# Filter bank and hardswish block on one core: small units run inside a last-stage chunk's matmuls, first-stage units in other steps, GpSimd's sums of x behind them

## The chip, the cores and the metric

One of the eight NeuronCores of a Trainium2 chip runs the kernel. The metric is the time of one execution on the device in microseconds (us), the median over repeated executions. The engines are called PE (TensorE), DVE (VectorE), ACT (ScalarE), POOL (GpSimd) and SP (SyncE); PEld is TensorE's loading of weights.

## The reference

```
X = np.fft.rfft(x, axis=1)                     # x: (8, 3008, 256) float32
Y = X * (filt_r + 1j * filt_i)[None, :, :]     # filter: (1505, 256)
y = np.fft.irfft(Y, n=3008, axis=1).reshape(24064, 256)
h = y @ w_in                                   # (256, 2048)
g = h * np.clip(h + 3.0, 0.0, 6.0) / 6.0
out = g @ w_out                                # (2048, 256)
```

## The kernel before

**The two halves of the work.** The Fourier part takes each of the 8 images (3008 rows of 256 values) as a 47 x 64 grid. A *first-stage* unit (`a_unit` for image 1, `a6_unit` for images 2 to 7) multiplies columns of the grid with a 47-point transform; its sums and differences go to DRAM (`z_tmp`). `t2_load` brings them back transposed, `b_unit` transforms along the 64, `f_unit` (three products on DVE) and `y_unit` (one subtraction and one addition on DVE) apply the filter, and `bi3_unit` transforms back along the 64 for three results `y` at a time and stores to DRAM (`g_tmp`). The *last stage* takes chunks of five columns (235 pairs of rows): `t4_load` brings a chunk, `n_five` multiplies it with the inverse 47-point transform, 40 small matmuls into two PSUM banks, and `ring` copies the result (ACT, L686) into a ring of three blocks, `xn`. The dense part takes blocks of 512 rows of the result, 47 of them, each in 8 steps of 256 of the 2048 hidden values.

**A step of the dense part.** From block 1 on both products are done with seven instead of eight block products. They need sums of x, which POOL makes once per block (`t_sums`, seven operations at L760, reading `xn`, when a chunk has completed the block), and sums of g, which DVE makes. A step is, in PE's order: product A11 into the bank `al` and S1, A12 into the bank `be` (`up_1`); two matmuls of the step before's down product; S2 into `al`, S4 into `be` (`up_2`); four down matmuls; S3 (`up_3`); four down matmuls; A22 into `al` (`up_5`); four down matmuls, of which the last two need `g_last`. ACT copies what was in `al` and `be` (L775, L776 in `up_1`, L785 in `up_2`, L804 in `up_5`) before the next product adds to it, and makes `relu(0)` and `relu(1)` (L809). DVE adds (L790, L795), makes g (`hswish`, L814, twice per step) and its sums (L821, L822, and `g_last`, L827). At a block's end `out_1` to `out_5` put the output together, with two operations in step 0 and three in step 1 on DVE, and one on POOL.

**Where the Fourier units stand.** PE, DVE, ACT, POOL and SP each take their instructions in the order in which the program records them. A table `plan` says which units a step holds, at one of three places: 0 (`EARLY`: after A12; among them `n_five` and `b_unit`), 1 (between the down matmuls before A22 and A22 itself; `a6_unit`, `bi3_unit`) and 2 (the end of the step: sums, stores, loads). A unit at place 1 may use `be`, because L790 has read it by then. For image n with first block `first[n]` (5, 11, 17, 23, 29, 35, 41), places are counted in steps from the beginning of block `first[n] - 5`; this count is called the offset here. The `bi3_unit`s of images 2 to 7 stand at offsets 11, 16, 27, 32, f_units at 2, 3, 6, 7, 12, 13 and 16 more, y_units at 4, 5, 10, 11, 14, 15 and 16 more, b_units with every other f_unit. The first-stage units stand in steps counted from two blocks earlier: `A_AT = (4, 6, 10, 12, 14, 15)`, five units of six columns and one (the last) of two. n_fives stand where the blocks need them, mostly in steps 0, 1, 4 and 6 of a block.

**Units on a quarter of the array.** `n_five`, `a6_unit` and `bi3_unit` use 48 to 64 rows and 64 columns of the array, so four of their matmuls occupy four quarters (two row halves, two column halves). An `a6_unit` of six columns and a `bi3_unit` are three rounds of four products of 256 columns into two PSUM banks of the pool `psF` and the bank `be`. The two row halves must not write the bank `be` at once; so DVE copies two elements from it after the first round (`tensor_copy(out=t[:, 2, 1, 0:2], ...)`, L483, and L601), and the second use of the bank waits for that copy. A float32 product stands in the profile as two weight loads and two matmuls, its two passes.

**Stages in time.** The stages of image n+1 run beside the dense part of image n, so nearly all the run is one sequence of steps with units in them. `late(i)` decides whether `g_last` comes before or after the up product's sums: after in steps 1 and 2 of a block and behind a step with a unit of `HEAVY`.

Of the kernel before, what the change touches and what calls it, by code (L numbers as in the profile page):

```python
# [37 lines left out]
HC = NC // 2  # L38
XC = 4
NB = HC // XC  # L40
SIX = tuple(range(0, HC, 6))
TC = 4
NT = KH // TC
TB = 3
# [138 lines left out]
def kernel(  # L183
# [198 lines left out]
    def x_at(b, c):  # L382
        if b == 1:
            return xs[:, (b * NB + c) % 3, :, :], c * XC, XC
        t = xs.rearrange("p i j d -> p (i j) d")
        return t[:, ds((b * len(SIX) + c) % 2 * 6, 6), :], SIX[c], min(6, HC - SIX[c])

    def x_load(b, c):
        t, c0, n_ = x_at(b, c)
# [70 lines left out]
    def a_sums(b, c):  # L460
# [5 lines left out]
        nc.vector.tensor_tensor(out=t[:, :, 1, :], in0=t[:, :, 0, :], in1=ps, op=ALU.subtract)  # L466
        nc.vector.tensor_tensor(out=t[:, :, 0, :], in0=t[:, :, 0, :], in1=ps, op=ALU.add)

    def a6_unit(b, c):
        xc, c0, n = x_at(b, c)  # L470
        n //= 2
        t = t3p.tile([P, 3, 2, D], FP32, name="t3") if n == 3 else t1p.tile([P, 2, 2, D], FP32, name="t1")
        banks = [psF.tile([P, 512], FP32, name="psf", tag="f") for h in range(2)]
        be = psU.tile([P, 512], FP32, name="be") if n == 3 else None
        for r in range(n):
            for g in range(2):
                for h in range(2):
                    j, ps, o = (2, be, h) if r == 2 - 2 * h and n == 3 else (r - h if n == 3 else 0,) + (banks[h], r - h if n == 3 else 0)
                    q = g * n + j
                    nc.tensor.matmul(ps[ts(g, 64), ts(o, D)], wa[ds(h * 64, NA), ds((c0 + q) * 2 * KH, 64)],  # L480
                                     xc[ds(h * 64, NA), q, :], start=True, stop=True)
            if n == 3 and r == 0:
                nc.vector.tensor_copy(out=t[:, 2, 1, 0:2], in_=be[:, D:D + 2])  # L483
        m = min(n, 2)
        two = [ps[:, 0:m * D].rearrange("p (j d) -> p j d", d=D) for ps in banks]
        nc.scalar.activation(out=t[:, 0:m, 0, :], in_=two[0], func=AXT.Copy)
        if n == 3:
                nc.scalar.activation(out=t[:, 2, 1, 2:D], in_=be[:, D + 2:], func=AXT.Copy)
        st["t1", b, c] = t, be, two[1], n

    def a6_sums(b, c):
        t, be, ps, n = st["t1", b, c]
        v, m = nc.vector, min(n, 2)
        if n == 3:
            v.tensor_tensor(out=t[:, 2, 0, :], in0=be[:, 0:D], in1=t[:, 2, 1, :], op=ALU.add)
            v.tensor_tensor(out=t[:, 2, 1, :], in0=be[:, 0:D], in1=t[:, 2, 1, :], op=ALU.subtract)
        v.tensor_tensor(out=t[:, 0:m, 1, :], in0=t[:, 0:m, 0, :], in1=ps, op=ALU.subtract)
        v.tensor_tensor(out=t[:, 0:m, 0, :], in0=t[:, 0:m, 0, :], in1=ps, op=ALU.add)

    def z6_store(b, c):  # L500
        t, _, _, n = st.pop(("t1", b, c))
        for g in range(2):
            for ri in range(2):
                p0 = g * 64 + ri * KH
                nc.gpsimd.dma_start(z_d[b, :, ri, ds(SIX[c] + n * g, n), :, :].rearrange("k j s d -> k (j s d)"),
                                    t[p0:p0 + KH, 0:n, :, :].rearrange("p j s d -> p (j s d)"))

    def z_store(b, c, q=nc.gpsimd):
# [80 lines left out]
    def bi3_unit(b, i):  # L589
        ys = [st.pop(("y", b, i + v)) for v in range(3)]  # L590
        c = psU.tile([P, 512], FP32, name="be")
        banks = [psF.tile([P, 512], FP32, name="psf", tag="f") for ri in range(2)]
        t = t3p.tile([P, 3, 2, D], FP32, name="t3")
        to = [t[:, q, :, :].rearrange("p u d -> p (u d)") for q in range(3)]
        for r in range(3):
            for v in range(2):
                for ri in range(2):
                    x, u, ps, o = (2, v, c, ri) if r == 2 * ri else (v, r - 1 + ri, banks[ri], r - 1 + ri)
                    nc.tensor.matmul(ps[ts(v, 64), ts(o, D)], wi[ts(ri, 64), 0, :], ys[x][ts(ri, 64), u, :], start=True, stop=True)  # L599
            if r == 0:  # L600
                nc.vector.tensor_copy(out=to[2][:, 0:2], in_=c[:, 0:2])  # L601
        nc.scalar.activation(out=to[1], in_=banks[1], func=AXT.Copy)
        st["t3", b, i] = t
        st["bi3"] = to[0], banks[0], to[2], c

    def bi3_copies():
        if "bi3" in st:
            to, ps, third, c = st.pop("bi3")
            nc.scalar.activation(out=to, in_=ps, func=AXT.Copy)
            nc.vector.tensor_copy(out=third[:, 2:512], in_=c[:, 2:512])  # L610
# [54 lines left out]
    def t4_load(i):  # L665
# [8 lines left out]
        for c in range(2):  # L674
            for hh in range(2):
# [2 lines left out]
                                  bass.AP(tensor=g_d.tensor, offset=g_d.offset + ((b * NC + j) * 2 + c) * KH * D,  # L678
                                          ap=[[D, KH], [-2 * KH * D, NJ], [1, D]]))

    def ring(i, a, m_, to, out, src):
        done = 0
        while done < m_:
            r = (chunks[i][0] * HC * NA + to + done) % RING
            m = min(m_ - done, RING - r)
            nc.scalar.activation(out=out(ds(r, m)), in_=src[:, :, ds(a + done, m)], func=AXT.Copy)  # L686
            done += m

    def ready(i):
        t, n = pair(i)  # L690
        if (t + n) // PAIRS > t // PAIRS > 0:
            t_sums(t // PAIRS)


    def n_five(i):
        b, js, o, n = chunks[i]
        s0 = i % 2 * NJ
        ps = [psF.tile([P, 512], FP32, name="psn", tag="f")[:, 0:2 * n].rearrange("p (e n) -> p e n", e=2) for c in range(2)]
        for q, j in enumerate(js):
            for dh in range(2):  # L700
                for g in range(2):
                    for c in range(2):
                        r = ds(c * HALF, ATOM)
                        nc.tensor.matmul(ps[c][ts(g, HALF), dh, ts(q, NA)], t4[r, s0 + q, ds(dh * P + g * HALF, HALF)],  # L704
                                         groups[r, j, :], start=True, stop=True)
# [267 lines left out]
    EARLY = (a_unit, b_unit, bi_unit, n_unit, n_five)  # L973

    def at(step, fn, *a):
        plan.setdefault((step, 0 if fn in EARLY else 1 if fn in (w_scale, bi3_unit, a6_unit) else 2), []).append((fn, a))

    with tc.manual_schedule():

# [134 lines left out]
        stored = 0  # L1114
# [34 lines left out]

        at(n_at[TAIL - 2] + 1, lambda: nc.sync.dma_start(edge, wai_d[:, ds(NW + ND, ND)]))  # L1150
# [2 lines left out]
        for n in range(1, B):  # L1153
            a_at, f_at, y_at, bi_at = places(n)
            for c, s in enumerate(a_at):
                at(s, a_unit if n == 1 else a6_unit, n, c)
# [24 lines left out]
        HEAVY = (f_unit, y_unit, a_sums, n_five, a6_sums, bi3_unit)  # L1181
# [106 lines left out]
```

## Time and profile before

| | |
|---|---|
| median of 4 runs | 2643.12 us (2641.83 to 2644.22) |
| the profiled execution | 2644.22 us, its span 2642.4 us |
| granted TensorE clock | 1.00 |
| DMA | 198.29 MB moved, mean 75 GB/s |
| PE po L843, the down products | 43% of the chain that ended last |
| PE al and be L764, the up products | 42% of the chain |
| PE psn L704, n_five | 2% of the chain |

The span is what the profiler saw of the program; the time of the execution holds some 2 us more. In the rows of a group the columns are line, engine, operation, tile written <- tiles read, shape and count, then busy time, mean ns of one, and idle time before them. The chain lists pieces of work in order of time, with start and length in us.

### The profile page before, as it was taken

The numbers are of one execution on the slowest core, as the hardware profiler recorded it, in microseconds if no ns is written. First come the engines' busy times: TensorE is split into PE (matmuls) and PEld (weight loads), VectorE is DVE, ScalarE is ACT, GpSimd is POOL, SyncE is SP. The second block draws the span as 40 slices with busy tenths as digits, with TensorE's granted clock in tenths as the row PEclk, the third lists the DMA queues.
The fourth block names the chain that finished last, engine by engine and source line by source line (L and its number), as shares of the span: only waits on it lengthen the run. The fifth ranks groups of instructions, "written<-read, shape, count | busy, mean of one in ns | idle before, by whom it ended". The sixth has DMA issues, their size and how long they took to land.

```text
span 2642.4 us, 54927 instructions
## 1 busy us (share of the span) xinstructions
PE 2625.9 (99%) x21920; PEld 2337.8 (88%) x21920; DVE 2047.5 (77%) x3611; ACT 1296.4 (49%) x2677; POOL 485.5 (18%) x711
## 2 busy tenths in 40 slices
PE   8999999999999999999999999999999999999999
PEld 6598988989889898889988898888988889999998
DVE  7878867887678876788767887688877878766666
ACT  4554454444544444444444444545445454454554
POOL 2242021120211102111021210211112120111110
PEclk9999999999999999999999999999999999999999
DMA  8732234112241132411233112331123311110000
GB/s 241 223 90 79 58 99 116 53 32 85 77 116 52 32 85 81 112 52 36 81 86 107 53 37 80 89 104 53 56 61 89 104 56 48 48 43 23 19 21 25
DMA packets 130710, 198.29 MB, mean 75 GB/s; under 512 B 21602, under 2 KB 97472, under 8 KB 130262
## 3 DMA queue, kind: packets, MB, share of 16 engines
q1 hardware_dynamic: 115165, 150.12, 20.5%
q0 software_dynamic: 14720, 44.16, 6.1%
q8 instruction: 173, 2.83, 0.4%
q14 instruction: 83, 0.68, 0.1%
q10 hardware_dynamic: 569, 0.50, 0.1%
HBM read 122.43 MB, written 83.98 MB: 78 GB/s over the span
## 4 chain that ended last, share of the span: by engine, by line
PE 96%; DMA 2%; DVE 1%; issue 0%; ACT 0%; SPq 0%; POOL 0%; POOLq 0%; DVEq 0%; ACTq 0%
PE po L843 43%; PE al L764 24%; PE be L764 18%; PE psn L704 2%; PE psf L539 1%; PE psf L480 1%; PE po L886 1%; PE psf L599 1%; PE be L599 1%; PE be L480 1%; DMA w_all<-in_x_dram 1%; DMA g_tmp<-t 1%; PE al L875 0%; PE be L875 0%; PE psf L453 0%; PE psn L715 0%
## 5 line engine op out<-in xcount | busy, mean ns | idle before, releaser
L843 PEld LDWEIGHTS po<-w_all,g 128*128 128x128 f32 x10276 | 1370.4, 191 | 106.9 <-issue 10.4
L843 PE MATMUL po<-w_all,g 128*128 128x128 f32 x10276 | 1393.9, 276 | 1.0 <-DVE g L814 0.6
L809 ACT ACTIVATE r<-h,half_c 128x512 f32<-128x512 f32 x736 | 531.0, 721 | 334.6 <-DVE h L790 322.5
L764 PE MATMUL al<-xt,w_all 128*128 128x256 f32 x2208 | 659.6, 381 | 0.1
L814 DVE SCALAR_TENSOR_TENSOR g<-r,h 128x512 f32<-128x512 f32 x736 | 534.1, 727 | 147.5 <-ACT r L809 132.3
L764 PE MATMUL be<-xt,w_all 128*128 128x256 f32 x1472 | 437.8, 379 | 0.0
L790 DVE TENSOR_TENSOR h<-be,s 128x512 f32<-128x512 f32 x368 | 253.7, 689 | 144.7 <-PE be L764 136.1
L764 PEld LDWEIGHTS al<-xt,w_all 128*128 128x128 f32 x2208 | 335.4, 192 | 1.0 <-issue 0.5
L760 POOL TENSOR_TENSOR xt<-xn 128x256 f32<-128x256 f32 x184 | 149.6, 833 | 905.6 <-ACT xn L686 871.7
L764 PEld LDWEIGHTS be<-xt,w_all 128*128 128x128 f32 x1472 | 279.7, 190 | 37.9
L804 ACT ACTIVATE h<-al 128x256 f32<-128x256 f32 x368 | 141.4, 384 | 297.2 <-PE al L764 297.2
L795 DVE TENSOR_TENSOR h<-al,s 128x256 f32<-128x256 f32 x368 | 156.1, 424 | 155.9 <-PE al L764 152.9
L822 DVE TENSOR_TENSOR g<-g 128x512 f32<-128x512 f32 x367 | 261.3, 712 | 12.6
L785 ACT ACTIVATE s<-al 128x256 f32<-128x256 f32 x368 | 141.4, 384 | 214.4 <-PE al L764 212.9
L764 PE MATMUL al<-xn,w_all 128*128 128x256 f32 x736 | 226.4, 389 | 0.0
L776 ACT ACTIVATE s<-be 128x256 f32<-128x256 f32 x368 | 141.4, 384 | 171.0 <-PE be L764 171.0
L764 PE MATMUL be<-xn,w_all 128*128 128x256 f32 x736 | 218.9, 379 | 0.0
L821 DVE TENSOR_TENSOR g<-g 128x256 f32<-128x256 f32 x367 | 165.0, 450 | 12.6
L775 ACT ACTIVATE s<-al 128x256 f32<-128x256 f32 x368 | 141.1, 383 | 64.8 <-PE al L764 64.8
L827 DVE TENSOR_TENSOR g<-g 128x256 f32<-128x256 f32 x367 | 160.2, 437 | 2.4
L764 PEld LDWEIGHTS be<-xn,w_all 128*128 128x128 f32 x736 | 139.8, 190 | 18.9
L764 PEld LDWEIGHTS al<-xn,w_all 128*128 128x128 f32 x736 | 111.4, 191 | 24.7 <-issue 22.3
(170 smaller groups left out, 1849.1 us busy)
## 6 DMA issues: line engine op xcount, KB each, us to landing
t<-g_tmp SPq DMA_DIRECT2D x184, 120.0 KB
t<-z_tmp SPq DMA_DIRECT2D x42, 512.0 KB
g_tmp<-t POOLq DMA_DIRECT2D x68, 256.0 KB, 4.3
z_tmp<-t POOLq DMA_DIRECT2D x120, 144.0 KB, 3.4
o_tmp<-o SPq DMA_DIRECT2D x46, 256.0 KB
xs<-in_x_dram SPq DMA_DIRECT2D x60, 192.0 KB
ft<-in_filt_r_dram SPq DMA_DIRECT2D x168, 64.0 KB
ft<-in_filt_i_dram SPq DMA_DIRECT2D x168, 64.0 KB
```

Source lines behind the costliest of these rows:

```text
L760: nc.gpsimd.tensor_tensor(out=o, in0=x0, in1=x1, op=op_)
L764: nc.tensor.matmul(ps, w_in[p][:, w, :], x, start=start, stop=stop, skip_group_check=True)
L776: nc.scalar.activation(out=s5, in_=be[:, 1, :], func=AXT.Copy)
L785: nc.scalar.activation(out=s[:, 1, :], in_=al, func=AXT.Copy)
L790: nc.vector.tensor_tensor(out=st["h"][0].rearrange("p (a n) -> p a n", a=2), in0=be, in1=s, op=ALU.add)
L795: nc.vector.tensor_tensor(out=st["h"][1][:, 256:512], in0=al, in1=s5, op=ALU.add)
L809: nc.scalar.activation(out=r, in_=st["h"][i], func=AXT.Relu, bias=half_c, scale=1.0 / 6.0)
L814: nc.vector.scalar_tensor_tensor(out=st["g", k, p][:, o:o + 2, :].rearrange("p a n -> p (a n)"), in0=st["r", i], scalar=1.0, in1=st["h"][i ...
L821: v.tensor_tensor(out=g[:, G1, :], in0=g[:, G3, :], in1=g[:, G22, :], op=ALU.add)
L822: v.tensor_tensor(out=g[:, G3:G2 + 1:2, :], in0=g[:, G3:G1 + 1, :], in1=g[:, G11:G11 + 1, :].broadcast_to([P, 2, 256]), op=ALU.subtract)
L827: nc.vector.tensor_tensor(out=g[:, G4, :], in0=g[:, G12, :], in1=g[:, G2, :], op=ALU.subtract)
L843: nc.tensor.matmul(st["po", k][bank][:, part, u, :], g[:, a, ts(u, P)], w_out[p][:, w, :], start=(p == 0 and n in OPENS and u == 0), stop= ...
```

## The change

A small unit is now one product per quarter of the array, two per row half: `a2_parts` (the two-column first-stage unit) and `bi1_parts` (one `y` instead of three). `five_and` records it inside an `n_five`: the unit's two products for one row half, beside eight of the chunk's products for the other half; then 24 of the chunk's products for both halves; then the unit's two products for the other half, beside the chunk's last eight. The unit's results go to the bank `be`, with DVE's two-element copy between its halves. Such a chunk stands at place 1 instead of 0. Its copies into `xn`, and for `bi1` one copy out of `be` on DVE, are recorded in `bi3_copies`, after A22 and `relu(1)`; `t_sums` is recorded there too, or, where the chunk stands in step 1 of a block (and no chunk three steps on), at place 2 three steps later.

The six-column units are now numbers 0 to 3 and 5 (`SIX`), the two-column one is number 4, at 12, with a chunk; numbers 3 and 5 stand at 13 and 15, which are steps 5 and 7 of a block. Of the four `bi3_unit`s of an image one is taken apart: single ones stand at offsets 9, 16 and 25 (image 6: 9, 16, 17; image 7: 9, 11, 16), those of three at 14 (image 7: 20), 27 and 32. Before, in images 2 to 7, all twelve `y` went in threes at 11, 16, 27 and 32. In all other `bi3_unit`s and in the `a6_unit`s the order of the products inside a round is changed: the two of one row half, then the two of the other.

```diff
...
-SIX = tuple(range(0, HC, 6))
+SIX = (0, 6), (6, 6), (12, 6), (18, 6), (24, 2), (26, 6)
...
+    def a_product(ps, g, o, xc, c0, q, h):
+        nc.tensor.matmul(ps[ts(g, 64), ts(o, D)], wa[ds(h * 64, NA), ds((c0 + q) * 2 * KH, 64)],
+                         xc[ds(h * 64, NA), q, :], start=True, stop=True)
     def a6_unit(b, c):
         xc, c0, n = x_at(b, c)
         n //= 2
-        t = t3p.tile([P, 3, 2, D], FP32, name="t3") if n == 3 else t1p.tile([P, 2, 2, D], FP32, name="t1")
+        t = t3p.tile([P, 3, 2, D], FP32, name="t3")
         banks = [psF.tile([P, 512], FP32, name="psf", tag="f") for h in range(2)]
-        be = psU.tile([P, 512], FP32, name="be") if n == 3 else None
+        be = psU.tile([P, 512], FP32, name="be")
         for r in range(n):
+            for h in (1, 0):
+                for g in range(2):
+                    j, ps, o = (2, be, h) if r == 2 - 2 * h else (r - h, banks[h], r - h)
+                    a_product(ps, g, o, xc, c0, g * n + j, h)
+            if r == 0:
+                nc.vector.tensor_copy(out=t[:, 2, 1, 0:2], in_=be[:, D:D + 2])
+        two = [ps.rearrange("p (j d) -> p j d", d=D) for ps in banks]
+        nc.scalar.activation(out=t[:, 0:2, 0, :], in_=two[0], func=AXT.Copy)
+        nc.scalar.activation(out=t[:, 2, 1, 2:D], in_=be[:, D + 2:], func=AXT.Copy)
+        st["t1", b, c] = t, be, two[1], n
+    def a2_parts(b, c):
+        xc, c0, n = x_at(b, c)
+        t = t1p.tile([P, 2, 2, D], FP32, name="t1")
+        be = psU.tile([P, 512], FP32, name="be")
+        st["t1", b, c] = t, be, None, 1
+        def part(h):
             for g in range(2):
-                for h in range(2):
-                    j, ps, o = (2, be, h) if r == 2 - 2 * h and n == 3 else (r - h if n == 3 else 0,) + (banks[h], r - h if n == 3 else 0)
-                    q = g * n + j
-                    nc.tensor.matmul(ps[ts(g, 64), ts(o, D)], wa[ds(h * 64, NA), ds((c0 + q) * 2 * KH, 64)],
-                                     xc[ds(h * 64, NA), q, :], start=True, stop=True)
-            if n == 3 and r == 0:
-                nc.vector.tensor_copy(out=t[:, 2, 1, 0:2], in_=be[:, D:D + 2])
-        m = min(n, 2)
-        two = [ps[:, 0:m * D].rearrange("p (j d) -> p j d", d=D) for ps in banks]
-        nc.scalar.activation(out=t[:, 0:m, 0, :], in_=two[0], func=AXT.Copy)
-        if n == 3:
-                nc.scalar.activation(out=t[:, 2, 1, 2:D], in_=be[:, D + 2:], func=AXT.Copy)
-        st["t1", b, c] = t, be, two[1], n
+                a_product(be, g, h, xc, c0, g, h)
+        def order():
+            nc.vector.tensor_copy(out=t[:, 0, 1, 0:2], in_=be[:, D:D + 2])
+        def copies():
+            nc.scalar.activation(out=t[:, 0, 1, 2:D], in_=be[:, D + 2:], func=AXT.Copy)
+        return 1, part, order, copies, lambda: None
...
         for r in range(3):
-            for v in range(2):
-                for ri in range(2):
+            for ri in range(2):
+                for v in range(2):
                     x, u, ps, o = (2, v, c, ri) if r == 2 * ri else (v, r - 1 + ri, banks[ri], r - 1 + ri)
                     nc.tensor.matmul(ps[ts(v, 64), ts(o, D)], wi[ts(ri, 64), 0, :], ys[x][ts(ri, 64), u, :], start=True, stop=True)
...
+    def bi1_parts(b, i):
+        y = st.pop(("y", b, i))
+        t = st["t3", b, i] = t1p.tile([P, 2, 2, D], FP32, name="t1")
+        be = psU.tile([P, 512], FP32, name="be")
+        to = t[:, 0].rearrange("p u d -> p (u d)")
+        def part(ri):
+            for v in range(2):
+                nc.tensor.matmul(be[ts(v, 64), ts(ri, D)], wi[ts(ri, 64), 0, :], y[ts(ri, 64), v, :], start=True, stop=True)
+        def order():
+            nc.vector.tensor_copy(out=to[:, 0:2], in_=be[:, 0:2])
+        def copies():
+            nc.vector.tensor_copy(out=to[:, 2:512], in_=be[:, 2:512])
+        return 0, part, order, lambda: None, copies
+    def g1_store(b, i):
+        t = st.pop(("t3", b, i))
+        for u in range(2):
+            nc.gpsimd.dma_start(g_d[b, :, :, 2 * i + u, :], t[ts(u, 64), 0])
     def bi3_copies():
+        if "five" in st:
+            for f in st.pop("five"):
+                f()
         if "bi3" in st:
...
+    sums_late = set()
...
-    def ready(i):
+    def ready(i, late=False):
         t, n = pair(i)
-        if (t + n) // PAIRS > t // PAIRS > 0:
+        if (t + n) // PAIRS > t // PAIRS > 0 and late == (i in sums_late):
             t_sums(t // PAIRS)
-    def n_five(i):
+    def n_five(i, parts=None, b_=0, x=0):
         b, js, o, n = chunks[i]
         s0 = i % 2 * NJ
         ps = [psF.tile([P, 512], FP32, name="psn", tag="f")[:, 0:2 * n].rearrange("p (e n) -> p e n", e=2) for c in range(2)]
-        for q, j in enumerate(js):
-            for dh in range(2):
-                for g in range(2):
-                    for c in range(2):
-                        r = ds(c * HALF, ATOM)
-                        nc.tensor.matmul(ps[c][ts(g, HALF), dh, ts(q, NA)], t4[r, s0 + q, ds(dh * P + g * HALF, HALF)],
-                                         groups[r, j, :], start=True, stop=True)
-        for c in range(2):
-            ring(i, 0, n, o, lambda at_: xn[:, :, c, at_], ps[c])
-        ready(i)
+        order = [(q, dh, g) for q in range(NJ) for dh in range(2) for g in range(2)]
+        def product_(c, q, dh, g):
+            r = ds(c * HALF, ATOM)
+            nc.tensor.matmul(ps[c][ts(g, HALF), dh, ts(q, NA)], t4[r, s0 + q, ds(dh * P + g * HALF, HALF)],
+                             groups[r, js[q], :], start=True, stop=True)
+        def both(a, b, n):
+            for i in range(n):
+                for c, o in ((0, a), (1, b)):
+                    product_(c, *order[o + i])
+        def rings():
+            for c in range(2):
+                ring(i, 0, n, o, lambda at_: xn[:, :, c, at_], ps[c])
+            ready(i)
+        if parts is None:
+            both(0, 0, len(order))
+            rings()
+            return
+        r, part, sync, copies, last = parts(b_, x)
+        part(r)
+        for m in range(8):
+            product_(1 - r, *order[m])
+        sync()
+        both(8 * r, 8 - 8 * r, 12)
+        part(1 - r)
+        for m in range(12, 20):
+            product_(r, *order[m])
+        copies()
+        st["five"] = last, rings
+    def five_and(*a):
+        n_five(*a)
...
-        plan.setdefault((step, 0 if fn in EARLY else 1 if fn in (w_scale, bi3_unit, a6_unit) else 2), []).append((fn, a))
+        plan.setdefault((step, 0 if fn in EARLY else 1 if fn in (w_scale, bi3_unit, a6_unit, five_and) else 2), []).append((fn, a))
...
-                at(s1, n_five, i)
+                five_at[s1] = i
...
-        A_AT = (4, 6, 10, 12, 14, 15)
+        BI_AT = {2: ((9, 0, 1), (14, 1, 3), (16, 4, 1), (25, 5, 1), (27, 6, 3), (32, 9, 3)),
+                 6: ((9, 0, 1), (14, 1, 3), (16, 4, 1), (17, 5, 1), (27, 6, 3), (32, 9, 3)),
+                 7: ((9, 0, 1), (11, 1, 1), (16, 2, 1), (20, 3, 3), (27, 6, 3), (32, 9, 3))}
+        A_AT = (4, 6, 10, 13, 12, 15)
         def places(n):
             if n == 1:
                 return (list(range(2, NB + 2)), [12, 13, 14, 18, 19, 20, 22, 23, 26, 27, 29, 31],
-                        [13, 15, 16, 19, 21, 22, 24, 25, 28, 30, 30, 32], [17, 24, 30, 34])
+                        [13, 15, 16, 19, 21, 22, 24, 25, 28, 30, 30, 32],
+                        [(17, 0, 3), (24, 3, 3), (30, 6, 3), (34, 9, 3)])
             k = first[n] * NP
             a_at = [k - 7 * NP + i for i in A_AT]
-            f_at, y_at, bi_at = ([k - (5 - 2 * r) * NP + i for r in range(2) for i in p]
-                                 for p in ((2, 3, 6, 7, 12, 13), (4, 5, 10, 11, 14, 15), (11, 16)))
+            f_at, y_at = ([k - (5 - 2 * r) * NP + i for r in range(2) for i in p]
+                          for p in ((2, 3, 6, 7, 12, 13), (4, 5, 10, 11, 14, 15)))
+            bi_at = [(k - 5 * NP + s, i, m) for s, i, m in BI_AT.get(n, BI_AT[2])]
+            y_at[5] += n == B - 1
             return a_at, f_at, y_at, bi_at
...
+                if n > 1 and SIX[c][1] == 2:
+                    with_five[s] = a2_parts, n, c
+                else:
+                    at(s, a_unit if n == 1 else a6_unit, n, c)
...
-                if i % 3 == 0:
-                    at(bi_at[i // 3], bi3_unit, n, i)
-                    at(bi_at[i // 3], g3_store, n, i)
                 at(y_at[i], y_unit, n, i)
+            for s, i, m in bi_at:
+                if m == 1:
+                    with_five[s] = bi1_parts, n, i
+                else:
+                    at(s, bi3_unit, n, i)
+                at(s, g3_store if m == 3 else g1_store, n, i)
...
+        for s, i in five_at.items():
+            if s in with_five and s % NP == 1 and s + 3 not in five_at:
+                sums_late.add(i)
+                at(s + 3, ready, i, True)
+            at(s, *((five_and, i) + with_five[s] if s in with_five else (n_five, i)))
+        HEAVY = (f_unit, y_unit, a_sums, n_five, five_and, a6_sums, bi3_unit)
...
```

More of the change, by code (lines that the diff above doesn't have):

```diff
@@ L385, in x_at @@
         t = xs.rearrange("p i j d -> p (i j) d")
-        return t[:, ds((b * len(SIX) + c) % 2 * 6, 6), :], SIX[c], min(6, HC - SIX[c])
+        return t[:, ds((b * len(SIX) + c) % 2 * 6, 6), :], *SIX[c]
     def x_load(b, c):
@@ L491, in a6_sums @@
     def a6_sums(b, c):
         t, be, ps, n = st["t1", b, c]
-        v, m = nc.vector, min(n, 2)
+        v, q = nc.vector, n - 1
+        v.tensor_tensor(out=t[:, q, 0, :], in0=be[:, 0:D], in1=t[:, q, 1, :], op=ALU.add)
+        v.tensor_tensor(out=t[:, q, 1, :], in0=be[:, 0:D], in1=t[:, q, 1, :], op=ALU.subtract)
         if n == 3:
-            v.tensor_tensor(out=t[:, 2, 0, :], in0=be[:, 0:D], in1=t[:, 2, 1, :], op=ALU.add)
-            v.tensor_tensor(out=t[:, 2, 1, :], in0=be[:, 0:D], in1=t[:, 2, 1, :], op=ALU.subtract)
@@ L497, in a6_sums @@
-        v.tensor_tensor(out=t[:, 0:m, 1, :], in0=t[:, 0:m, 0, :], in1=ps, op=ALU.subtract)
-        v.tensor_tensor(out=t[:, 0:m, 0, :], in0=t[:, 0:m, 0, :], in1=ps, op=ALU.add)
+            v.tensor_tensor(out=t[:, 0:2, 1, :], in0=t[:, 0:2, 0, :], in1=ps, op=ALU.subtract)
+            v.tensor_tensor(out=t[:, 0:2, 0, :], in0=t[:, 0:2, 0, :], in1=ps, op=ALU.add)
     def z6_store(b, c):
@@ L504, in z6_store @@
                 p0 = g * 64 + ri * KH
-                nc.gpsimd.dma_start(z_d[b, :, ri, ds(SIX[c] + n * g, n), :, :].rearrange("k j s d -> k (j s d)"),
+                nc.gpsimd.dma_start(z_d[b, :, ri, ds(SIX[c][0] + n * g, n), :, :].rearrange("k j s d -> k (j s d)"),
                                     t[p0:p0 + KH, 0:n, :, :].rearrange("p j s d -> p (j s d)"))
@@ L1113 @@
             in_block.setdefault(pair(i)[0] // PAIRS, []).append(i)
-        stored = 0
+        stored, five_at, with_five = 0, {}, {}
         for i in range(2, len(chunks)):
@@ L1155 @@
             for c, s in enumerate(a_at):
-                at(s, a_unit if n == 1 else a6_unit, n, c)
+                if n > 1 and SIX[c][1] == 2:
+                    with_five[s] = a2_parts, n, c
+                else:
+                    at(s, a_unit if n == 1 else a6_unit, n, c)
                 at(s, a_sums if n == 1 else a6_sums, n, c)
@@ L1177 @@
             prev = a_at
-        HEAVY = (f_unit, y_unit, a_sums, n_five, a6_sums, bi3_unit)
+        assert set(with_five) <= set(five_at), sorted(set(with_five) - set(five_at))
+        for s, i in five_at.items():
[4 more added lines that the diff above has]
+        HEAVY = (f_unit, y_unit, a_sums, n_five, five_and, a6_sums, bi3_unit)
         def late(i):
```

## The prediction, made before the changed kernel was run

> **What bounds the kernel now.** I read the page first: busy shares, then the chain that ended last.
>
> ```profile
> PE 2625.9 (99%) x21920; PEld 2337.8 (88%) x21920; DVE 2047.5 (77%) x3611; ACT 1296.4 (49%) x2677; POOL 485.5 (18%) x711
> PE 96%; DMA 2%; DVE 1%; issue 0%; ACT 0%; SPq 0%; POOL 0%; POOLq 0%; DVEq 0%; ACTq 0%
> ```
>
> TensorE is the clock of everything. So I price each unit by what it adds to a step: the time between the `be` products that open two steps, in the chain of waits of two stretches.
>
> ```profile
> 731.33 0.86 PE be L764 x4
> ...
> 739.21 0.86 PE be L764 x4
> ...
> 743.60 0.59 PE psf L480 x8
> ...
> 746.14 0.86 PE be L764 x4
> ...
> 752.29 0.86 PE be L764 x4
> ```
> ```profile
> 476.71 0.86 PE be L764 x4
> 477.57 1.31 PE psn L704 x80
> ...
> 484.36 0.86 PE be L764 x4
> ...
> 490.51 0.86 PE be L764 x4
> ...
> 498.37 0.86 PE be L764 x4
> ```
>
> By these differences, to the ns from the matmuls' own starts: a step with no unit (746.14 and 484.36) takes 6.148 us; with a six-column a6_unit 7.880 (+1.732); with the two-column one 6.937 (+0.789); with n_five 7.657 (+1.509); with bi3_unit 7.857 (+1.709). The costs add (n_five with bi3_unit: 9.365) and repeat within a few ns in nearly all steps: VectorE, ScalarE and GpSimd are hidden there, and I must look for where the change ends that.
>
> **What is removed, and the price of a merged unit.** Per image 2 to 7 one bi3_unit (1.709) and the two-column a6_unit (0.789) go: 6 x 2.498 = 15.0 us. Added: 24 small units (18 bi1, 6 a2) inside an n_five. The timeline shows n_five as 20 rounds of four quarter-array matmuls 58.4 ns apart (47 columns would stream faster; each quarter waits for its own 64-column weights). A small unit gives every quarter one product of 256 columns, two passes of 0.216 us. In the new order all four quarters get 20 x 58.4 ns + 0.432 us, so the merged stretch should be 0.432 longer than n_five, if quarters run independently; a long first pass starts slower (0.267 for 0.216, a five 0.079 for 0.058), so I take 0.45. Bounds: 0.40 (weights load under the long passes, a shorter exit) and 0.789 (all the standalone cost stays). 24 x 0.45 = 10.8; net **-4.2 us** (bounds -5.4 and +3.9).
>
> Do the quarters run independently? Row first, the third round of a bi3_unit:
>
> ```profile
> 933.02 0.13 PEld L599 LDWEIGHTS psf<-y,wi 64*64 64x64 f32 x1
> 933.03 0.13 PEld L599 LDWEIGHTS be<-y,wi 64*64 64x64 f32 x1
> ```
> ```profile
> 933.03 0.43 PE L599 MATMUL be<-y,wi 64*64 64x256 f32 x1
> ...
> 933.24 0.38 PE L599 MATMUL psf<-y,wi 64*64 64x256 f32 x1
> ```
>
> The first product's second weights load at 933.02, ahead of the `be` product that waits for VectorE; yet its second pass runs at 933.24, 0.2 us after that later product began. So a pass queued at one quarter does not hold the others. The Trainium skill (TensorE: Matmul & The Clock Gate, Part 3) says the opposite, that matmuls start and end strictly in program order. By that rule the eight passes of a small unit would stand in a row, 8 x 0.216 = 1.73 us for 0.45, an estimate of +31 us in all. I follow the row.
>
> The `be` bank's second half waits for VectorE's two-element copy. In an a6_unit that round trip is 0.945 us from the unit's start (1008.51 to 1009.45); here the second half starts about 1.15 us in, so it costs nothing while VectorE is free. Queued behind that wait on TensorE are the last eight products and A22; behind the copy on VectorE stands L814, as in a bi3_unit today.
>
> **Row halves in turn** (bi3_unit, a6_unit): the two waiting products now come last of their round, and the first half's are done sooner. From the starts above: 0.026 us for each of 30 a6_units, about 0.01 for 22 bi3_units: **-1.0** (bounds 0 and -1.5).
>
> **Copies of xn move behind relu(1).** Before, n_five stood early in its step and ScalarE copied (L686) with time to spare. Merged, the two copies are queued after the last L809 and ahead of the next step's L775. A bi3_unit shows that spot:
>
> ```profile
> 826.26 0.72 ACT L809 ACTIVATE r<-h,half_c 128x512 f32<-128x512 f32 x1
> 826.89 0.58 ACT L609 ACTIVATE t<-psf 128x512 f32<-128x512 f32 x1
> 827.37 0.38 ACT L775 ACTIVATE s<-al 128x256 f32<-128x256 f32 x1
> ```
>
> The next `be` product is at 826.97 (call it N). L609 starts at N-0.08; L775, normally at N+0.20, at N+0.40. Two xn copies of 0.565 (0.46 apart) put L775 at N+0.84, its end at N+1.22. S2 writes the same bank, normally at N+1.31; after such a wait the matmul follows 0.15 us later (the row of 311.96 below), so 0.07 late. A chunk that wraps round the ring has four copies, 0.11 us longer: 0.18 late. 17 x 0.07 + 5 x 0.18 = **+2.1** (bounds 0 and +5); the other two merges precede a b_unit.
>
> **GpSimd's sums start later.** They start 0.08 us after the last xn copy: today 3.5 us into the step of the n_five, merged at N+1.0 of the *next* step (1.14 where a chunk wraps), and run 5.7 us. The three steps of delay do not hold GpSimd: after an image's first merge (step 1 of a block) the built order has only g1_store between, and a queue knows no steps. Only where a bi3_unit's store stands between (the merge at offset 25) do the sums start later: three steps on, 3.1 us after that step's N, when the last store issue there ends today. What sums do to VectorE:
>
> ```profile
> 590.88 0.80 DVE L827 TENSOR_TENSOR g<-g 128x256 f32<-128x256 f32 x1
> 591.61 1.21 DVE L814 SCALAR_TENSOR_TENSOR g<-r,h 128x512 f32<-128x512 f32 x1
> ```
> ```profile
> 590.67 1.59 POOL L760 TENSOR_TENSOR xt<-xt 128x256 f32<-128x256 f32 x2
> 592.23 1.18 POOL L760 TENSOR_TENSOR xt<-xn 128x256 f32<-128x256 f32 x1
> ```
>
> Alone L827 takes 0.415, L814 0.69, a sum 0.73. Here they take turns, each waiting out the other less 0.14. Operations with a PSUM operand (L790, L795, L923) keep their length. A unit-free step has 0.5 us of slack on VectorE, and its `g` must be ready 2.01 us after N: at 311.81 an L814 ended, at 311.96 the matmul started, where 2.17 is normal. By queue:
> - Step after the first merge (y_unit in it; images 2 to 6), in us after N: L822, ready at 1.23, runs 1.73 to 2.42; L827, ready 4.22, 4.37 to 4.79; L814, ready 4.7, 5.24 to 5.93; the y operations (0.69 each) 6.38 to 7.07 and 7.52 to 8.21. The step is 6.33 long (6.148 + 0.18), so the next L814 ends at 8.21 - 6.33 + 0.71 = 2.59, 0.58 late. 5 x 0.58 = 2.9.
> - Offset 25 (images 2 to 5; step with b_unit and f_unit, 7.365 long): L814, ready 5.59, runs 6.13 to 6.82, the three f products end at 8.83, the next L814 at 2.22: 4 x 0.21 = 0.8.
> - Merges before a b_unit (image 6's third, image 7's second): 0.5 together.
> - Step after a step-0 merge: L827 ends at N+4.84, needed at 5.11: nothing, 0.3 each if a turn goes the other way.
> - Step 5 after an a2: the sums of a6 read PSUM: nothing.
>
> Together **+4.2** (bounds 0 and +12). The n_fives that cost 0.04 to 0.09 more for this reason today (7.718 at 585.0) lose it: **-0.4**.
>
> **What moves and stays hidden.** Last z6_store now six columns: its first issue goes from N-0.16 to N+1.40 of step 0, and t2_load (SP queue, with table_load and t4_load behind it) lands 4.1 to 8.6 us before its b_unit: 2.5 left at worst. The z store of an a2 waits behind the sums, 7 us; its next reader is that same t2_load, three steps on. x_load of column block 5 has 12 us for landings of 2.4 to 5.4. bi1 stores are six issues for four, 0.5 to 0.7 us each, on a GpSimd 18% busy; g_tmp is read blocks later. The POOL addition of out_4 slips a step behind the sums after step 0, and SP's store with it; `o` has two buffers. Copies out of `be` have the times of bi3's and a6's third column, which cause no wait. The remaining n_fives keep their place.
>
> **Sum.** -4.2 - 1.0 - 0.4 + 2.1 + 4.2 = +0.7. The profiled execution took 2644.22 us (span 2642.4 and 1.8 around it), 1.1 above the median 2643.12 of the runs shown; so 2644.9 for that execution, **2643.8** on the median. No change that can be told: 0.2% (5.3 us) is about what a measurement of this kernel can tell.
>
> **Rivals.**
> - *The new waits don't reach TensorE* (0.19): ScalarE's copies start earlier or the turns fall well: -5.6, and with 0.40 per merge -6.8: 2636 to 2638. For: 2.01 and 1.31 are margins missed by tenths. Against: the ScalarE order is fixed by the code.
> - *VectorE falls behind* (0.22, slower): each of 22 displaced groups of sums can delay up to seven operations by 0.59 us, 4.1 us where a unit-free step hides 0.5. It decides once L814 ends later than N+2.01; half a microsecond more per group is +11: 2655. For: y_unit and f_unit steps are full already (6.24 us of VectorE work in 6.148). Against: PSUM operations let the sums pass.
> - *Quarters wait for each other* (0.09, slower): at the standalone 0.789 per merge 2652; if the long passes of one half shut out the other, twice 0.43 more each (1.31), 2664.
> - *The sums do wait three steps*, as the change says: then the 2.9 goes, 2641, still no change (inside the 0.50 of the forecast). Against: nothing in the queue to hold them.
>
> **How the numbers follow.** Forecast 0.50, within 2638.5 to 2648; faster 0.19; slower 0.22 + 0.09 = 0.31. Range: down into the first rival (2637), up through most of the second (2653).
>
> **What would show it.** Right: merged steps near 8.1 us (7.657 + 0.45); L775 at N+0.8 after them; S2 0.07 late; sums from N+1.0 of the next step; a 0.6 us gap ahead of L843 two steps after each image's first merge; bi3 steps at 7.85, a6 at 7.85. Wrong: merged steps above 8.3 (quarters not independent) or below 8.05; no gaps on L843; any TensorE wait on DMA in images 2 to 7.

## The result, and the profile after

The changed kernel takes 2646.45 us (median of 41 runs, 2645.43 to 2649.57) against 2642.92 for the kernel before (61 runs): ratio 1.0014, 95% interval 1.001 to 1.0019, 3.5 us slower. That lies inside the range, and the change is smaller than the 0.2% that the prediction took for the limit of what can be told; with this many runs the interval is 0.05% either way, so the 3.5 us are clear of the noise. The median is 2.7 us above the number forecast, and the parts of the sum show why.

The profiled execution took 2646.40 us, its span 2644.6. The spans of the two profiled executions differ by only 2.2 us, because the stretch ahead of the first step took 129.3 us in the one of before and 127.6 in this one; over the eleven profiled executions of this study that stretch varies between 126.7 and 129.3. So I compare the 367 steps of the dense part, from the first `be` product to the last, below called the *sum of steps*: 2498.58 us before, 2502.41 after, **+3.83**. Nearly all unchanged steps repeat within a few ns (those whose n_five runs beside GpSimd's sums within 0.02 us). Step 7.1 is step 1 of block 7; steps are counted from 0. Step lengths, and times after N, are taken from the matmuls' own starts. The chain shows the same `be` product 0.16 us later, since there a piece counts from the end of the piece before it.

The page after, busy shares and the chain:

```profile
PE 2625.5 (99%) x21920; PEld 2349.6 (89%) x21920; DVE 2066.1 (78%) x3641; ACT 1282.3 (48%) x2665; POOL 500.5 (19%) x723
PE 95%; DVE 3%; DMA 1%; issue 0%; ACT 0%; SPq 0%; DVEq 0%; POOL 0%; POOLq 0%; ACTq 0%
```

TensorE's busy time is 0.4 us less than before, but VectorE's share of the chain went from 1% to 3%. (Once the chain has left TensorE it counts all of VectorE's time back to the last wait, so this is more than the time lost.) The chain around image 2's first merge (step 7.1) shows both sides:

```profile
474.46 0.86 PE be L833 x4
...
482.64 0.86 PE be L833 x4
...
486.33 0.42 DVE h L864
486.76 0.41 DVE g L896
487.17 1.13 DVE g L883
...
488.33 1.11 DVE y L588
...
489.47 1.11 DVE y L589
...
490.68 0.70 DVE g L883
491.38 0.04 issue
491.42 1.16 PE po L912 x8
...
495.66 0.86 PE be L833 x4
```

The merged step takes 8.174 us. In the next two steps the chain leaves TensorE at 486.33 and returns at 491.42: everything between is VectorE, with operations of 0.69 us that last 1.1. GpSimd's rows of the timeline beside the two y operations:

```profile
487.71 1.17 POOL L829 TENSOR_TENSOR xt<-xn 128x256 f32<-128x256 f32 x1
488.97 1.05 POOL L829 TENSOR_TENSOR xt<-xt 128x256 f32<-128x256 f32 x1
```

The two L883 are the ones worked out in the prediction: the second ends 2.59 us after its step's `be` product, which starts at 488.78 (forecast 2.59), and the step takes 0.57 us longer (forecast 0.58).

Step 38.1, in image 7, has the one large gap where the prediction expected none: it put the sums' cost at nothing in every step behind a merge in step 0. The step takes 8.257 us where four of the other five such steps take 6.185, and the fifth, 32.1, which holds a merge of its own, 8.211 (0.04 over a merged step). Its chain, then ScalarE's timeline at its beginning (N = 2177.21):

```profile
2176.98 0.42 DVE o L983
...
2177.42 0.70 DVE y L588
...
2178.14 0.70 DVE y L589
...
2178.93 1.04 DVE g L883
...
2180.00 0.84 DVE g L890
...
2182.68 1.16 PE po L912 x8
```
```profile
2176.50 0.72 ACT L878 ACTIVATE r<-h,half_c 128x512 f32<-128x512 f32 x1
2177.13 1.00 ACT L730 ACTIVATE xn<-psn 128x470 f32<-128x470 f32 x2
2178.02 0.38 ACT L844 ACTIVATE s<-al 128x256 f32<-128x256 f32 x1
2178.28 0.40 ACT L845 ACTIVATE s<-be 128x256 f32<-128x256 f32 x1
```

The output's operation L983 and a y_unit (L588, L589) stand ahead of L883, which starts only at N+1.72, when the sums have begun (N+1.00). ScalarE's rows are as forecast: two copies of xn, then L844 at N+0.81 (forecast 0.84).

### The profile page after: what moved, and what is told of

It reads as the page before. It is cut to its first block, busy times and chain, and to the rows that moved or that the text cites. A ratio compares the mean times of both kernels' runs of the same rounds, so it can differ in the third digit from the quotient of the medians.

```text
span 2644.6 us, 54934 instructions
## 1 busy us (share of the span) xinstructions
PE 2625.5 (99%) x21920; PEld 2349.6 (89%) x21920; DVE 2066.1 (78%) x3641; ACT 1282.3 (48%) x2665; POOL 500.5 (19%) x723
## 4 chain that ended last, share of the span: by engine, by line
PE 95%; DVE 3%; DMA 1%; issue 0%; ACT 0%; SPq 0%; DVEq 0%; POOL 0%; POOLq 0%; ACTq 0%
PE po L912 43%; PE al L833 24%; PE be L833 17%; PE psn L747 2%; PE psf L556 1%; PE po L955 1%; PE psf L470 1%; PE be L470 1%; DVE g L883 1%; PE psf L616 1%; PE be L616 1%; DMA w_all<-in_x_dram 0%; PE al L944 0%; PE be L944 0%; PE po L565 0%
## 5 line engine op out<-in xcount | busy, mean ns | idle before, releaser
L883 DVE SCALAR_TENSOR_TENSOR g<-r,h 128x512 f32<-128x512 f32 x736 | 534.3, 727 | 158.1 <-ACT r L878 142.3
L829 POOL TENSOR_TENSOR xt<-xn 128x256 f32<-128x256 f32 x184 | 155.1, 869 | 448.8 <-ACT xn L730 448.8
L989 POOL TENSOR_TENSOR o<-p,o 128x256 f32<-128x256 f32 x46 | 37.3, 811 | 783.9 <-ACT s L854 451.3
L844 ACT ACTIVATE s<-al 128x256 f32<-128x256 f32 x368 | 141.3, 384 | 61.0 <-PE al L833 61.0
```

The costliest lines, as they stand in the source:

```text
L829: nc.gpsimd.tensor_tensor(out=o, in0=x0, in1=x1, op=op_)
L883: nc.vector.scalar_tensor_tensor(out=st["g", k, p][:, o:o + 2, :].rearrange("p a n -> p (a n)"), in0=st["r", i], scalar=1.0, in1=st["h"][i ...
```

## The experiments

Sums of steps are given beside medians, since they tell tenths of a microsecond apart.

**1. The order of the row halves alone** (kernel before; the same swap in `bi3_unit`):

```diff
-            for g in range(2):
-                for h in range(2):
+            for h in (1, 0):
+                for g in range(2):
```

> The kernel before with one part of the change alone: the order of the products inside a round (one row half, then the other) in all bi3_units and a6_units. By the steps of the changed kernel's trace: 0.048 us for each of 30 six-column a6_units and 0.024 for each of 28 bi3_units, 2.1 us less: 2640.8 us. By the prediction's own figures (0.026 and 0.01): 1.1 less, 2641.8 us.

Measured 2640.8 us, sum of steps 2.13 below before: 0.048 us for an a6_unit, 0.024 for a bi3_unit, as read from the changed kernel and about twice the prediction's figures. The medians alone don't tell this from nothing (ratio 0.9993, 0.9984 to 1.0002); the steps do. This part of the change is a small gain by itself. In the changed kernel, with 22 of the 28 bi3_units left, it is worth 2.0 us, so the rest of the change costs 3.83 + 2.0 = 5.8 us.

**2. The place and the order of the copies alone, without small units** (kernel before):

```diff
+        AT_1 = [8 * k + 1 for k in (7, 9, 13, 15, 19, 21, 25, 27, 31, 32, 37)]
...
-                at(s1, n_five, i)
+                at(s1, five_late if s1 in AT_1 else n_five, i)
```
(`five_late` is `n_five` at place 1, with its `ring` copies and `ready` in `bi3_copies`.)

> The kernel before, no small units; only 11 chunks that stand alone in step 1 of a block (blocks 7, 9, 13, 15, 19, 21, 25, 27, 31, 32, 37) move from place 0 to place 1, with their copies into xn behind relu(1) and the sums right behind them. Theory (place and order make the waits, the small units have no part in them): the step itself takes 7.657 us (so all of 0.517 in a merged step is the small unit's own); S2 is 0.16 us late after the 5 chunks that wrap round the ring and 0.04 after the others (1.0 us in all); a gap of 0.57 us ahead of the first down product two steps after each of 9 chunks that has a y_unit one step on (5.1), 0.7 after block 32's; 0.4 is saved in the steps themselves; total +6 us, 2649 us. Rival (the small unit's copy out of be and its stores make VectorE and GpSimd late): only S2's 1.0 us, 2643.5 us.

Measured 2650.01 us; sum of steps +6.84. The moved chunk's step takes 7.654 us (n_five at place 0: 7.657), so all of the 0.517 in a merged step is the small unit's. And the waits are there without any small unit: S2 late by 0.158 us behind wrapping chunks and 0.037 behind others, 0.57 us two steps after the first chunk of an image, 0.69 after its second, 0.68 in 32.3. Its chain in steps 7.2 and 7.3 has the same operations, with the same lengths within 0.02 us, as the changed kernel's:

```profile
486.44 1.13 DVE g L824
...
487.61 1.12 DVE y L571
...
488.75 1.11 DVE y L572
...
489.96 0.70 DVE g L824
...
490.70 1.16 PE po L853 x8
```

The theory holds: moving eleven chunks in this way costs about 7 us with nothing merged into them. The price is not the same everywhere as in the changed kernel. Behind an image's second chunk (9.1 and its like) it is 0.69 us here and 0.18 there, because there the sums stand behind a bi3_unit's stores and start only in step 9.4 (607.95), where here they start in 9.2 (591.94).

**3. The copies ahead of relu(1):**

```diff
-        st["five"] = last, rings
+        rings()
+        st["five"] = last,
```

> The changed kernel with the copies into xn (and the sums, where they follow at once) recorded at the end of five_and, ahead of A22 and relu(1), in place of behind them. Theory (ScalarE's order makes S2 late, and the late start of the sums makes the rest): the copies start about 6.3 us into the merged step in place of 8.1, the second product S2 of the next step is late no more (0.037 us in 17 steps and 0.158 in 5, 1.4 us in all), and the sums start some 0.9 us sooner, which takes about half of the 0.57 us from the gaps two steps after a first merge (5 of them); total 2643 to 2645 us. Rival (the two copies now stand ahead of the copy of al and of relu(1), and push them by 0.25 us, so g comes late instead): no gain, 2646.5 us or more.

Measured 2659.83 us, 13.4 above the changed kernel; sum of steps +12.57. Of the theory, two things came true: the 0.037 us of late S2 and the 0.57 us gaps are gone. But the rival holds, and at a far higher price than it named. The chain of its step 7.1 and the start of 7.2:

```profile
481.43 0.49 ACT xn L730 x2
...
481.94 0.63 ACT xn L730 x2
482.57 0.29 ACT h L874
...
482.88 0.73 ACT r L879
...
483.63 2.49 DVE g L884
...
486.15 0.84 DVE g L891
```

The copies push the copy of `al` (L874) from 7.05 to 7.58 us into the step. The next product into that bank starts 0.05 us after the copy ends (482.90), so TensorE waits 0.29 us in each merged step with a bi1 (8.459 for 8.174; 0.13 more where the chunk wraps) and 0.34 in those with an a2. And relu(1) ends late, so that L884 meets the sums already running: it ends after 2.48 us and three sums, and step 7.2 takes 7.52 us for 6.31, four others like it the same. The order that the change chose, with copies behind relu(1), is the better one.

**4. Image 7's sixth y_unit:**

```diff
-            y_at[5] += n == B - 1
+            y_at[5] += 2 * (n == B - 1)
```

> The changed kernel with one line of it altered: the sixth y_unit of image 7 stands in step 38.1 in place of 38.0 (it can't go back to 37.7, since its buffer is free only after the small unit of 38.0). Theory (the 2.1 us that step 38.1 takes too long come from this y_unit, whose two operations on VectorE begin the step just when GpSimd's sums of x begin to take turns with VectorE): step 38.1 falls from 8.257 to 6.19 us, the length of the other five steps that follow a merged chunk in step 0 of a block, and 38.2 stays at 7.365, since its b_unit stands ahead of the first down product; total 2646.45 - 2.1 = 2644.4 us. Rival (sums and the output operations of that step overrun VectorE whether or not a y_unit is there): 7.2 us or more in 38.1, total 2645.4 or more.

Measured 2645.24 us; sum of steps 1.85 below the changed kernel. Step 38.1 falls to 6.183, and 38.2 gets 0.26 longer, which was not expected. The y_unit made the gap of 2.1 us. The plainer trial, with the y_unit back at 37.7 as before, gives no time: there are three buffers for `y`, and at 37.7 the y_unit would wait for one that only the small unit of 38.0, recorded behind it, frees, so such a program can't end.

**5. Sums that really wait three steps:**

```diff
...
+        if late:
+            nc.gpsimd.tensor_copy(out=p_wait, in_=st["up"][3][:, 0:2])
```

> The changed kernel, in which the sums that stand three steps behind their chunk really wait three steps: ahead of them GpSimd copies two elements of s5, a tile that ScalarE writes 1.4 us into that step. Theory (the 0.57 us gaps two steps after an image's first merge come from where the sums run, beside a y_unit in steps without other units): the sums run from 1.5 us into the step of the b_unit, the five gaps go (2.9 us), and five such as at offset 25 (0.18 us in the step after the b_unit) come, 0.9 us at most; total 2644.4 us. Rival (VectorE lacks the time wherever the sums run): the gaps move along with the sums at their full size, total 2646 us or more.

Measured 2648.16 us; sum of steps +1.37. The theory fails, the rival holds: the five gaps of 0.57 in the third step are gone, and five of 0.69 stand in the fifth (and 1.5 us in 32.4 and 32.5 for 0.68 in 32.3). The sums now start 1.65 us into the step with b_unit and f_unit (7.4), stretch L886 to 1.21 us, and the three products of the f_unit queue behind it ahead of the next L886:

```profile
501.41 1.21 DVE g L886
502.62 0.60 DVE s L578
...
503.24 0.68 DVE s L579
...
503.93 0.69 DVE s L580
...
504.66 0.70 DVE g L886
...
505.41 0.60 PE po L915 x3
```

**6. The y_units moved ahead of the sums:**

```diff
+            y_at[2] = k - 5 * NP + 8
+            y_at[3] = k - 5 * NP + 9
```
(and image 7's sixth as in 4)

> The changed kernel with y_units moved and all else kept: the third and fourth of each of images 2 to 7 stand at offsets 8 and 9 in place of 10 and 11, ahead of the sums that follow the first merge, and image 7's sixth at 38.1. Theory (a gap needs both, the sums and a y_unit, in one step; in a step without other units VectorE takes the sums with 0.5 us to spare): the five gaps of 0.57 us two steps after a first merge go (2.9 us), and the 2.1 us of step 38.1 turn to 0.26 in step 38.2 as in the run before; total 2646.45 - 4.7 = 2641.8 us. Rival (the sums alone make g late): 0.3 us or more stays in each of the five steps, total 2643.5 us or more.

Measured 2647.15 us; sum of steps +0.77. Half of the theory holds: with the y_units gone from there, step 7.3 and its like take 6.15 us; there is no gap, though the sums run in the same place. But the total rises, for a reason that neither side had: the third y_unit now stands at the end of step 0 of a block, behind the output's two operations and ahead of L883, and six merged steps take 9.14 us for 8.174:

```profile
472.75 0.69 DVE o L978
...
473.54 0.42 DVE o L983
...
473.98 0.70 DVE y L588
...
474.70 0.70 DVE y L589
...
475.49 0.70 DVE g L883
...
478.09 1.16 PE po L912 x8
```

Here no sums run at all: GpSimd has no operation between 467.6 and 477.8. At a block's end VectorE had no room for a y_unit even without them.

**7. The row halves not mixed:**

```diff
         part(r)
-        for m in range(8):
-            product_(1 - r, *order[m])
         sync()
-        both(8 * r, 8 - 8 * r, 12)
+        both(0, 0, 20)
         part(1 - r)
-        for m in range(12, 20):
-            product_(r, *order[m])
```

> The changed kernel without the mixing of row halves: the small unit's products for one half, the chunk's twenty rounds for both halves in the old order, the unit's products for the other half. Theory A (a pass that waits at one quarter doesn't hold those of the other quarters, as far as they are queued): the half that is free runs ahead, 8.17 us as before, total 2646.5 us. Theory B (the products pass in the order of the program, so the other half stands still beside the unit's passes, twice 0.43 us): 8.60 us, 24 x 0.43 = 10.4 us, total 2657 us. In between, some rounds can be queued ahead, and the difference tells how many.

Measured 2654.46 us; merged steps 8.467 (bi1) and 8.454 (a2) us, 0.29 and 0.26 more than mixed, where theory B said 0.43 and A nothing. TensorE's timeline of one:

```profile
858.68 0.43 PE L631 MATMUL be<-y,wi 64*64 64x256 f32 x2
858.70 0.33 PE L747 MATMUL psn<-wai,t 48*64 48x47 f32 x4
858.95 0.38 PE L631 MATMUL be<-y,wi 64*64 64x256 f32 x2
859.17 0.27 PE L747 MATMUL psn<-wai,t 48*64 48x47 f32 x4
```

The free half runs one product (two passes) on each of its quarters beside the long ones, then stands still until 859.17, when the long passes are over. So a waiting pass does not hold the other quarters at once, but only one product per quarter ran ahead: the mixing in the program's order is what fills them. Strict program order of matmuls, the rule that the prediction weighed at +31 us, is not what these rows show, since products recorded later ran between the two passes of an earlier one.

**8. The small unit's second half sooner:**

```diff
-        both(8 * r, 8 - 8 * r, 12)
+        both(8 * r, 8 - 8 * r, 9)
         part(1 - r)
-        for m in range(12, 20):
+        for m in range(9, 17):
             product_(r, *order[m])
+        both(17, 17, 3)
```

> The changed kernel with the small unit's second half three rounds sooner: nine rounds of the chunk for both row halves in place of twelve, the second half beside eight products, then the last three rounds for both. Theory (of the 0.517 us that a merged step takes over one with n_five alone, 0.432 are the two passes that each quarter of the array gets, and the rest is that the long passes come last: A22 starts 0.267 us after the last of them and only 0.161 after the last short pass of an n_five): merged steps fall from 8.174 to 8.07 us, 24 x 0.1 = 2.4 us, total 2644.0 us. Rival (the rest is lost where the unit begins and where long and short passes meet): 8.17 us as before, 2646.4 us.

Measured 2646.31 us; merged steps 8.169 for 8.174. The rival holds: the 0.085 above two passes is not lost at the end. Where exactly it is lost stays open; a first long pass holds its quarter 0.267 us for 0.216, which may be 0.05 of it; no run tried that.

**9. The a2 merge without the bi1 merges:**

```diff
-        BI_AT = {2: ((9, 0, 1), (14, 1, 3), (16, 4, 1), (25, 5, 1), (27, 6, 3), (32, 9, 3)),
...
+        BI_AT = {2: ((11, 0, 3), (16, 3, 3), (27, 6, 3), (32, 9, 3))}
...
-            y_at[5] += n == B - 1
```

> The changed kernel without the small bi1 units: all twelve y of an image go in threes at offsets 11, 16, 27 and 32 as before, image 7's y_unit stays at 37.7; only the two-column first-stage unit is merged with a chunk, with the new order of the first-stage units and of the row halves. Theory (the bi1 merges earn 1.685 - 3 x 0.517 = 0.13 us an image and pay over 1 us for their waits; the a2 merge earns 0.789 - 0.535 and pays 0.037): 6 x 0.217 = 1.3 us below the kernel with the row halves alone (2640.8), that is 2639.5 us, the fastest so far. Rival (the first-stage units in steps 5 and 7 and the sums behind the a2 cost what they earn): 2640.8 us or more.

Measured 2639.80 us, ratio to before 0.9988 (0.9979 to 0.9997): the lowest median here. The runs of experiment 1 (2639.62 to 2643.37) and these (2638.77 to 2641.94) overlap, but the sum of steps is 1.25 below that of experiment 1 (expected 1.3), so the a2 merges pay. The bi1 merges, with all that their places move (image 7's y_unit among it), are what made the change slower: 2502.41 - 2495.21 = 7.2 us.

## Why the prediction was right, and where its sum was off

The outcome (no change beyond 0.2%) was right, and so were most of the waits by place and size. The sum was 3.1 us too low. Two terms make that up: step 38.1 (+2.1) and the merges ahead of a b_unit (+1.0). Three other errors, +1.7, -1.0 and -0.7, cancelled, and that is luck. Measured values are read from the step lengths of the two traces; their sum is of unrounded values:

| term | predicted | measured |
|---|---|---|
| units removed | -15.0 | -15.0 |
| 24 merges | +10.8 | 18 x 0.517 + 6 x 0.535 = +12.5 |
| row halves in turn | -1.0 | 30 x 0.048 + 22 x 0.024 = -2.0 |
| n_fives relieved | -0.4 | -0.4 |
| S2 late | +2.1 | 17 x 0.037 + 5 x 0.158 = +1.4 |
| two steps after an image's first merge | +2.9 | +2.9 |
| offset 25 | +0.8 | 4 x 0.177 = +0.7 |
| merges before a b_unit | +0.5 | 0.01 + 0.68 + 0.13 + 0.73 = +1.5 |
| step 38.1 | nothing | +2.1 |
| sum | +0.7 | +3.8 |

**Right.** Independent quarters (experiment 7, within a short queue); ScalarE's order and its 0.04 to 0.16 us on S2; sums that begin 0.7 to 1.0 us into the next step (1.00 where the chunk does not wrap) and don't wait three steps; where VectorE's lag reaches the down product, and by how much (within 0.04 us), in nine places: five steps behind a first merge and four at offset 25. Experiment 2 shows that the late S2 and the waits behind a first merge come from the chunk's place and its late copies alone.

**The term that was left out: step 38.1, 2.1 us.** The prediction's line "Step after a step-0 merge: ... nothing" covers this step and holds for the other five, but the y_unit that the diff moves in image 7 (`y_at[5] += n == B - 1`) from step 37.7 to the end of 38.0, so that its two operations run in 38.1, has no line in the working. It was moved because its buffer is held until the small unit of 38.0, and it came to stand behind the output's operations and ahead of L883. Experiment 4 shows it.

**Terms mis-sized.** A merge costs 0.517 to 0.535, not 0.45: +1.7. The two merges ahead of a b_unit were put at 0.5 together and measured 1.5: the three products of the f_unit queue behind a stretched L883, the same pattern as in experiment 5. The prediction gave no working for its 0.5. The chain of 37.4 and 37.5:

```profile
2148.64 1.21 DVE g L883
2149.86 0.60 DVE s L577
...
2150.47 0.68 DVE s L578
...
2151.17 0.69 DVE s L579
...
2151.89 0.70 DVE g L883
...
2152.64 1.16 PE po L912 x8
```

On the other side the row halves gave twice what was forecast, and S2 is late by less: in 7.2 it starts 0.05 us after L844 ends, not 0.15. Experiment 8 refuted my explanation of the 0.07 per merge (long passes at the end).

**A rival priced wrongly.** "The sums do wait three steps" was put at 2641. Experiment 5 made them wait and got slower (2648.16 us): there was no better place three steps on. The +31 us for strict program order does not follow from the order alone: eight passes stand in a row only if passes on different quarters can't overlap, and in the rows of experiment 7 they do.

**Rivals.** VectorE did fall further behind than forecast, in 38.1 and ahead of the b_units, 3.1 us in all, but not behind each group of sums, as the rival of 2655 had it. In the mixed order the quarters did not hold each other for long: a merge cost 0.517 to 0.535 us, of which 0.432 are its own passes. The waits did reach TensorE.

## What to carry to other kernels

When TensorE is 99% busy, a merge that saves TensorE time must be priced together with everything its place moves on the other engines: here the merges of the bi1 kind saved TensorE 0.13 us an image and made the kernel 7.2 us slower, while the plain reordering of the row halves gave 2.1. (Nearly all of the 7.2 us are waits that follow from the moved chunks and the moved y_unit.) Go through the diff line by line for operations that move for the sake of buffers; one y_unit moved by one step cost 2.1 us, more than all the late second products together (1.4). A delay written in a plan is no delay in a queue: the sums ran up to two steps ahead of their place in the plan. And where a queue is full, a gap may only move, as it did in experiments 5 and 6: move one thing and look where the gap goes.

## What the hardware did that I had not expected

- VectorE and GpSimd do not always take turns one by one: an L884 that became ready while sums ran back to back lasted 2.48 us, three sums of 0.8 us, where in the other rows shown a turn makes at most 1.2 of 0.69 (experiment 3).
- The row halves of the array ran apart by one product per quarter, then the free half started nothing for 0.39 us (858.78 to 859.17, experiment 7).
- Letting the two products of one row half follow each other saved 0.048 us per a6_unit, twice what the starts of the single products had suggested; why it is so much was not tried.
